# The first loads of weights issued behind the first pair's queries, keys and values

## The chip, the core and the metric

One Trainium2 chip, and on it one core. The metric is the time of one execution of the whole program on the device, in microseconds (us). The core's engines are TensorE (PE, with its weight loads as PEld), VectorE (DVE), ScalarE (ACT), GpSimd (POOL) and SyncE (SP); SP issues every transfer of this kernel.

## What is computed

A layer of attention with a memory beside it, and a gated layer of experts' size behind it, all in 32-bit floats:

```
a     = softmax(mask(q k^T / 8));  local = a v                 # B=4, H=8, S=576, D=64
q_p   = phi(q);  mem = (q_p M_prev) / (q_p z_prev + 1e-6)      # phi(x) = max(x + 1, exp(min(x, 0)))
x     = sigmoid(beta) * mem + (1 - sigmoid(beta)) * local      # -> 2304 x 512
out   = (sigmoid(x w_gate) * (x w_val)) w_out                  # 512 -> 1536 -> 512
```

## The kernel before

The 2304 rows of x are worked in six groups of 384. For each group, attention is computed for four pairs of heads, in three items each; the first group takes the tails (192 queries) of two batches, so a pair of it has two loads of queries and keys (`kp`), two of values (`vt` or `vr`) and shares two tiles of the memory (`mb`). The expert layer of a group (`moe`) runs over 12 blocks f of 128 hidden columns, and while it runs the attention of the next group is woven into it.

The weights arrive as 64-bit numbers. For a block f three raw tiles of 512 KB (`wr`, three buffers) are loaded, and `convert` turns each into a high and a low 32-bit part: one operation on ACT (line 603), four on DVE (604, 606, 609, 612), a copy on ACT (223) and a subtraction on DVE (233). One result stays in `wg`, a tile per f; the other two go to `sv`, which has three buffers, and are also written to `w` in device memory, from where later groups load them. So the conversion of 36 raw tiles goes on beside the attention and the experts of group 0, and f+3 needs an `sv` buffer that the experts' block f has left.

Every operation is first recorded with its engine and its dependences (`Program.add`), and `issue` then orders them: it plays the program with costs from a table and gives each engine, whenever it is free, the ready operation with the lowest number `order`. That number is the place at which the operation was recorded, less a lead from the table `LEAD`: loads and stores of weights on SP have a lead of 200. The order on each engine is fixed when the kernel is built; on the chip, each engine takes its instructions in that order and waits at one whose inputs are not there. The first block's weights are recorded inside the first attention pair (behind its eighth step), the second's behind the 22nd, the others from inside `moe`. The first pair's recorded operations begin with the loads of `kp` (numbers 4 and 5), `bt`, `vt`, the next pair's `kp` and the `mb` tiles (18 to 22, with POOL's clearing of them between).

Of the kernel before, what the change touches and what calls it, by code (L numbers as in the profile page):

```python
# [25 lines left out]
COLD = 12.0  # L26

LEAD = {("attention", "pe"): 150, ("weights", "sp"): 200}

WAKE = {  # L30
    "act": {"act": 0.14, "dve": 0.13, "pe": 0.26, "pool": 0.2, "sp": 0.14},
# [7 lines left out]
class Program:  # L39
# [24 lines left out]
    def add(self, engine, cost, emit, reads=(), writes=(), kb=0):  # L64
        i = len(self.ops)
        deps = set()
        for k in (*reads, *writes):
            if k[:2] in self.touched:
                use, ops = self.touched[k[:2]]
                assert use == k[2], f"{k} is read or written after its buffer went to a new use"  # L70
                if k in writes and k not in self.writer:
                    deps.update(self.before[k[:2]])
                ops.add(i)
        for k in reads:
            if k in self.writer:
                deps.add(self.writer[k])
        for k in writes:
            if k in self.writer:
                deps.add(self.writer[k])
            deps.update(self.readers.pop(k, ()))  # L80
        for k in reads:
            self.readers.setdefault(k, set()).add(i)
        for k in writes:
            self.writer[k] = i
        deps.discard(i)
        order = (i if self.turn is None or engine != "pe" else self.turn) - LEAD.get((self.part, engine), 0)
        self.ops.append((engine, cost, kb, emit, deps, order))

    @contextmanager
# [712 lines left out]
```

## Time and profile before

| | |
|---|---|
| median of 3 runs | 687.88 us (686.35 to 690.77) |
| the profiled execution | 686.17 us, its span 684.4 us |
| PE busy / PEld busy | 663.3 us (97%) / 582.0 us (85%) |
| DVE / ACT / POOL busy | 363.1 / 334.3 / 8.1 us |
| granted clock of TensorE, mean | 0.999 |
| moved | 122.20 MB, mean 179 GB/s |

The span is the time between the first and the last recorded instruction. The busy share of PE is a mean over all stages; PE's ends are modelled, so that short waits between matmuls don't appear as idle time. Rows of a timeline start with the start in us and the length in us; a row in brackets at the end tells how long the engine was idle before and what released it. SPq rows are SP's issues of transfers, not the transfers themselves.

### The profile page before, as it was taken

Reading aid. Unit: us, or ns where it says so; the run is one execution under the profiler, and the core shown is the slowest. Engines: PE = TensorE matmul, PEld = TensorE weight load, DVE = VectorE, ACT = ScalarE, POOL = GpSimd, SP = SyncE. Lnnn points to the kernel's source line nnn. Section 1 sums busy time; section 2 is a strip of 40 time slices with the busy share of each in tenths; the row PEclk is TensorE's granted clock in tenths of the full one; section 3 lists DMA queues with packets and bytes.
Section 4 is the critical chain, followed back from the end, with each engine's and each line's share of the span. In section 5 each row is a group of like instructions: output and inputs, shape, how many; then the busy total and the mean of one; then the engine's idle time right before and its main releaser. Section 6 shows DMA issues by size and latency. Waiting matters only on the chain.

```text
span 684.4 us, 12496 instructions
## 1 busy us (share of the span) xinstructions
PE 663.3 (97%) x4992; PEld 582.0 (85%) x4992; DVE 363.1 (53%) x995; ACT 334.3 (49%) x656; POOL 8.1 (1%) x52
## 2 busy tenths in 40 slices
PE   4999999999999999999999999999999999999996
PEld 2556688887799999899999999989998899999995
DVE  6799889898864443454444345454445533111111
ACT  6678656557663553553454454354644624121111
POOL 2000000000000000000000000000000000000000
PEclk9999999999999999999999999999999999999999
DMA  8677757877644543543444634543622331554541
GB/s 280 238 260 239 231 157 260 271 235 267 230 153 162 178 169 140 197 155 136 167 147 143 266 117 162 180 168 125 241 102 92 134 124 63 185 186 167 185 168 63
DMA packets 31946, 122.20 MB, mean 179 GB/s; under 512 B 7568, under 2 KB 9616, under 8 KB 22672
## 3 DMA queue, kind: packets, MB, share of 16 engines
q1 hardware_dynamic: 31888, 121.41, 51.1%
q8 instruction: 39, 0.64, 0.4%
q14 instruction: 19, 0.16, 0.1%
HBM read 104.09 MB, written 17.30 MB: 177 GB/s over the span
## 4 chain that ended last, share of the span: by engine, by line
PE 90%; ACT 5%; DMA 2%; DVE 1%; issue 1%; SPq 1%; POOL 0%; ACTq 0%
PE bank L210 70%; PE bank L214 10%; PE bank L217 7%; PE bank L472 4%; ACT a L493 1%; ACT kq L223 1%; DMA vt<-in_vp_dram 1%; ACT at L223 1%; DMA kp<-in_qk_dram 1%; SPq L241 1%; DVE a L484 0%; ACT wt L603 0%; DMA out_dram<-ob 0%; ACT ob L704 0%; DVE xs L233 0%
## 5 line engine op out<-in xcount | busy, mean ns | idle before, releaser
L210 PE MATMUL bank<-xh,sv 128*128 128x384 f32 x576 | 169.4, 347 | 0.1
L210 PE MATMUL bank<-xh,wg 128*128 128x384 f32 x576 | 166.0, 343 | 0.3
L210 PE MATMUL bank<-sv,gh 128*128 128x512 f32 x432 | 142.6, 407 | 0.0
L689 DVE SCALAR_TENSOR_TENSOR th<-th,bank 128x384 f32<-128x384 f32 x72 | 39.8, 553 | 145.3 <-PE bank L210 130.7
L210 PEld LDWEIGHTS bank<-xh,wg 128*128 128x128 f32 x576 | 105.1, 188 | 7.8 <-issue 2.9
L210 PEld LDWEIGHTS bank<-xh,sv 128*128 128x128 f32 x576 | 105.8, 188 | 3.7 <-issue 1.8
L493 ACT ACTIVATE a<-a,st 128x512 f32<-128x512 f32 (+4 forms) x144 | 79.8, 581 | 44.7 <-DVE st L484 43.7
L687 ACT ACTIVATE th<-bank 128x384 f32<-128x384 f32 x72 | 35.3, 490 | 133.8 <-PE bank L210 133.5
L210 PE MATMUL bank<-xl,sv 128*128 128x384 f32 x288 | 98.0, 340 | 0.0
L210 PE MATMUL bank<-xl,wg 128*128 128x384 f32 x288 | 98.0, 340 | 0.0
L484 DVE CUSTOM_DVE_ANT_0 a<-bank,mask 128x512 f32<-128x512 f32 (+4 forms) x144 | 66.5, 485 | 55.6 <-PE bank L210 49.3
L210 PEld LDWEIGHTS bank<-sv,gh 128*128 128x128 f32 x432 | 78.0, 188 | 13.1 <-issue 0.7
L210 PE MATMUL bank<-sv,gl 128*128 128x512 f32 x216 | 87.4, 405 | 0.0
L217 PE MATMUL bank<-idn,a 128*128 128x128 f32 x400 | 73.2, 278 | 3.8 <-ACT a L493 2.8
L223 ACT COPY at<-bank 128x512 f32<-128x512 f32 (+1 forms) x120 | 59.1, 514 | 34.7 <-PE bank L217 34.6
L223 ACT CAST gh<-th 128x384 fp32r<-128x384 f32 x72 | 36.9, 512 | 62.9 <-DVE th L689 62.2
L217 PEld LDWEIGHTS bank<-idn,a 128*128 128x128 f32 x400 | 49.7, 142 | 15.0 <-ACT a L493 4.9
L210 PEld LDWEIGHTS bank<-xl,wg 128*128 128x128 f32 x288 | 54.2, 188 | 3.0 <-issue 0.5
L223 ACT CAST kq<-kp 64x768 fp32r<-64x768 f32 (+1 forms) x76 | 48.2, 638 | 16.4 <-PE bank L210 15.2
L210 PEld LDWEIGHTS bank<-xl,sv 128*128 128x128 f32 x288 | 54.2, 188 | 1.0 <-issue 0.7
L472 PE MATMUL bank<-kp 64*128 64x512 f32 (+5 forms) x156 | 42.1, 494 | 9.4 <-DMA kp<-in_qk_dram 8.4
L233 DVE TENSOR_TENSOR gl<-th,gh 128x384 fp32r<-128x384 f32 x72 | 39.9, 554 | 20.5 <-ACT gh L223 20.1
(62 smaller groups left out, 693.2 us busy)
## 6 DMA issues: line engine op xcount, KB each, us to landing
sv<-w SPq DMA_DIRECT2D x60, 1024.0 KB, 4.8
wr<-in_w_dram SPq DMA_DIRECT2D x36, 512.0 KB, 4.4
kp<-in_qk_dram SPq DMA_DIRECT2D x32, 384.0 KB, 4.8
w<-sv SPq DMA_DIRECT2D x12, 1024.0 KB, 4.8
out_dram<-ob SPq DMA_DIRECT2D x16, 256.0 KB, 4.4
vt<-in_vp_dram SPq DMA_DIRECT2D x8, 330.0 KB, 4.1
vr<-in_vp_dram SPq DMA_DIRECT2D x8, 330.0 KB, 5.7
vt<-in_vp_dram SPq DMA_DIRECT2D x8, 198.0 KB, 3.2
```

Of the source, the lines that this page charges most:

```text
L210: lambda: nc.tensor.matmul(out=out, lhsT=lhsT, rhs=rhs, start=start, stop=stop), r, w)
L214: lambda: nc.tensor.matmul(out=out, lhsT=lhsT, rhs=rhs, start=start, stop=stop), r, w)
L217: pe(0.110, lambda: nc.tensor.transpose(out=out, in_=in_, identity=identity), r, w)
L223: act(n, lambda: nc.scalar.copy(out=out, in_=in_), r, w)
L233: dve(n, lambda: nc.vector.tensor_tensor(out=out, in0=in0, in1=in1, op=op), r, w)
L241: pg.add("sp", 0.5, lambda: nc.sync.dma_start(out=out, in_=in_), r, w, kb)
L472: pe(2 * m / 2385.0, lambda kp=kp, j=j, r=r, q=q, m0=m0, m1=m1: nc.tensor.matmul(out=sp[j][0][m0:m1, :m], lhsT=kp[r, u.qa + q:u.qa + q + m ...
L484: dve(m + 60, lambda aj=aj, sj=sj, pj=pj: nc.vector.tensor_tensor_reduce(out=aj[:, k0:k1], in0=pj[:, :m], in1=mk, scale=-0.125, scalar=3.0 ...
L493: act(W, lambda aj=aj, sj=sj: nc.scalar.activation(out=aj[:, :W], in_=aj[:, :W], func=AF.Exp, scale=-1.0, bias=sj[:, len(ns) - 1:len(ns)], ...
L687: act(GT, lambda: nc.scalar.activation(out=th, in_=pg_[:, :GT], func=AF.Tanh, scale=0.5), [pg_k], [th_k])
L689: dve(GT, lambda: nc.vector.scalar_tensor_tensor(out=th, in0=th, scalar=1.0, in1=pv[:, :GT], op0=ALU.add, op1=ALU.mult,), [th_k, pv_k], [t ...
```

## The change

A lower bound is put on the number that orders loads and stores of weights on SP. Before, the lead of 200 made the numbers of the first block's loads negative, and they stood ahead of every other transfer. Now no such number is below 21, which is the number of the third of the four loads of the `mb` tiles.

```diff
 LEAD = {("attention", "pe"): 150, ("weights", "sp"): 200}
+
+FIRST = 21
@@ Program.add
         deps.discard(i)
+        first = FIRST if (self.part, engine) == ("weights", "sp") else -1000
         order = (i if self.turn is None or engine != "pe" else self.turn) - LEAD.get((self.part, engine), 0)
+        order = max(order, first)
         self.ops.append((engine, cost, kb, emit, deps, order))
```

Nothing else of the source changes; line numbers behind `Program.add` grow by four. Since `issue` plays the whole program, the order on all engines moves.

On SP, the start of the program. `wr` are the raw weights, `kp` queries and keys, `bt` the gate's numbers, `vt` values. A wait on DMAHW is one for an earlier transfer to have landed: there are eight such counters, and a transfer waits for the one eight places ahead of it. Before:

```order
L241 DMA wr_129<-in_w_dram 128x1024
L241 DMA wr_131<-in_w_dram 128x1024
L241 DMA wr_133<-in_w_dram 128x1024
L241 DMA kp_101<-in_qk_dram 128x768
L241 DMA kp_102<-in_qk_dram 128x768
L241 DMA bt<-in_beta_dram 128x8
L241 DMA vt_103<-in_vp_dram 128x660
L241 DMA vt_104<-in_vp_dram 128x660
L241 DMA kp_105<-in_qk_dram 128x768 [waits DMAHW0_49]
```

The same place of the changed kernel, from its first transfer on:

```order
L245 DMA kp_101<-in_qk_dram 128x768
L245 DMA kp_102<-in_qk_dram 128x768
L245 DMA bt<-in_beta_dram 128x8
L245 DMA vt_103<-in_vp_dram 128x660
L245 DMA vt_104<-in_vp_dram 128x660
L245 DMA kp_105<-in_qk_dram 128x768
L245 DMA kp_106<-in_qk_dram 128x768
L245 DMA mb_107<-in_mz_dram 64x4x65 [waits Pool_49]
L245 DMA mb_107<-in_mz_dram 64x4x65 [waits DMAHW0_49]
L245 DMA mb_108<-in_mz_dram 64x4x65 [waits DMAHW1_49,Pool_49]
L245 DMA wr_129<-in_w_dram 128x1024 [waits DMAHW2_49]
L245 DMA wr_131<-in_w_dram 128x1024 [waits DMAHW3_49]
```

The three loads of raw weights went from the first three places to the 11th to 13th; the last quarter of `mb` and the next pair's values follow them.

On DVE, its first instructions. `wt` is the working tile of a conversion; rows 484 (488 after) read the first scores out of a bank. Before:

```order
L604 TENSOR_SCALAR wt_130<-wt_130 128x512
L606 TENSOR_SCALAR wt_130<-wt_130 128x512
L609 SCALAR_TENSOR_TENSOR wt_130<-wr_129,wt_130 128x512
L612 SCALAR_TENSOR_TENSOR wt_130<-wr_129,wt_130 128x512
L604 TENSOR_SCALAR wt_132<-wt_132 128x512
...
L612 SCALAR_TENSOR_TENSOR wt_132<-wr_131,wt_132 128x512
L606 TENSOR_SCALAR wt_134<-wt_134 128x512
L484 ISA a_112,st_114<-bank_63,mask 128x512
```

In the changed kernel DVE begins with that last row, and its first conversion stands behind the first pair's first two items (from the 14th row on):

```order
L488 ISA a_123,st_124<-bank_70,mask 128x320
...
L488 ISA a_123,st_124<-bank_64,mask_73,st_124 128x256
L488 ISA st_124 128x1
L608 TENSOR_SCALAR wt_130<-wt_130 128x512
L610 TENSOR_SCALAR wt_130<-wt_130 128x512
L488 ISA a_113,st_114<-bank_68,mask 128x512
L488 ISA st_114 128x1
L488 ISA a_118,st_115<-bank_69,mask 128x512
L488 ISA st_115 128x1
L613 SCALAR_TENSOR_TENSOR wt_130<-wr_129,wt_130 128x512
```

Eleven rows of conversion went from ahead of the first score to between the scores of the first pair and behind them.

On PE, the first products with the memory (`mb`, with the features `ph`) among the scores (`kp`) and transposes (`idn`). Before:

```order
L472 MATMUL bank_64<-kp_102 64x256
L217 MATMUL bank_66<-idn,a_118 128x128 x4
L217 MATMUL bank_67<-idn,a_119 128x128 x3
L214 MATMUL bank_65<-mb_107,ph_109 128x130
L217 MATMUL bank_67<-idn,a_119 128x128
L472 MATMUL bank_68<-kp_105 128x512
```

After:

```order
L476 MATMUL bank_70<-kp_102 64x320
L218 MATMUL bank_65<-mb_107,ph_109 128x130
L476 MATMUL bank_63<-kp_102 64x320
L476 MATMUL bank_64<-kp_101 64x256
L476 MATMUL bank_64<-kp_102 64x256
L221 MATMUL bank_66<-idn,a_118 128x128 x4
```

The product with `mb` stands about ten matmuls earlier. From the experts' first block of group 1 on, all engines have the same order in both kernels (on DVE from just behind the 36th and last conversion).

## Rows read from the trace of the kernel before

**Rows 1.** The page, part 1: busy time, share of span and instructions of each engine.

```profile
PE 663.3 (97%) x4992; PEld 582.0 (85%) x4992; DVE 363.1 (53%) x995; ACT 334.3 (49%) x656; POOL 8.1 (1%) x52
```

**Rows 2.** Busy time by stretch: stretch, length, engines' busy us, granted clock, DMA share, GB/s.

```profile
0.00:5.50 5.50, 0.00 (x0) 0.00 (x0) 0.00 (x0) 1.94 (x2) 4.43 (x20) 1.00 0.66 212
5.50:14.00 8.50, 5.15 (x14) 2.33 (x15) 8.35 (x23) 5.29 (x11) 0.24 (x2) 1.00 0.91 328
14.00:30.00 16.00, 14.65 (x108) 8.53 (x108) 11.82 (x37) 12.07 (x25) 0.23 (x2) 1.00 0.82 269
30.00:60.00 30.00, 28.73 (x325) 17.48 (x322) 27.68 (x86) 23.44 (x47) 0.47 (x4) 1.00 0.67 225
60.00:100.00 40.00, 38.39 (x420) 30.34 (x416) 33.94 (x98) 24.73 (x51) 0.59 (x5) 1.00 0.66 210
100.00:172.50 72.50, 71.60 (x455) 59.69 (x452) 66.79 (x162) 47.00 (x92) 0.22 (x2) 1.00 0.76 253
172.50:200.00 27.50, 27.28 (x225) 22.93 (x226) 19.80 (x57) 17.16 (x34) 0.22 (x2) 1.00 0.65 226
200.00:684.40 484.40, 477.55 (x3468) 440.67 (x3467) 194.75 (x537) 202.65 (x399) 1.69 (x15) 1.00 0.43 153
```

**Rows 3.** Waits of PE, first 60 us: line, waited for, us, times, longest.

```profile
PE bank L472 <- DMA kp<-in_qk_dram: 8.4, 1, 8.4
```

**Rows 4.** Timeline, first 10 us: SP's first issues, and who starts when they land.

```profile
0.73 1.35 SPq L241 DMA_DIRECT2D wr<-in_w_dram  x3
2.13 1.14 SPq L241 DMA_DIRECT2D kp<-in_qk_dram  x2
4.82 0.66 ACT L603 ACTIVATE wt<-wr 128x512 f32<-128x512 f32 x1 [2.81 <-DMA wr<-in_w_dram]
6.07 0.67 ACT L603 ACTIVATE wt<-wr 128x512 f32<-128x512 f32 x1 [0.59 <-DMA wr<-in_w_dram]
8.38 3.79 PE L472 MATMUL bank<-kp 64*128 64x512 f32 x8 [8.38 <-DMA kp<-in_qk_dram]
9.40 0.34 PEld L472 LDWEIGHTS bank<-kp 64*128 64x128 f32 x2 [0.51 <-DMA kp<-in_qk_dram]
```

**Rows 5.** Loads of kp, first 30 us, six of them: from issue to landing.

```profile
DMA to landing us min/median/max: 3.5/6.4/9.0
```

**Rows 6.** Timeline, DVE: its first instruction, and the first score.

```profile
5.51 0.43 DVE L604 TENSOR_SCALAR wt<-wt 128x512 f32<-128x512 f32 x1 [5.51 <-ACT wt L603]
11.05 0.68 DVE L484 CUSTOM_DVE_ANT_0 a<-bank,mask 128x512 f32<-128x512 f32 x1
```

**Rows 7.** Transposes on PE by shape, from 8 to 14.2 us, then 14.2 to 30 us.

```profile
L217 PE MATMUL bank<-idn,a 128*128 128x128 f32 x7 | 1.8, 423 | 0.5 <-POOL vt L374 0.5
...
L217 PE MATMUL bank<-idn,a 128*128 128x128 f32 x35 | 5.3, 287 | 1.3 <-ACT a L493 1.3
```

**Rows 8.** The conversions' last operation on DVE, first 200 us: duration, first and last start.

```profile
L612 DVE SCALAR_TENSOR_TENSOR wt<-wr,wt x36: 651/684/697, 7.2 to 174.4; 128x512 int32<-128x512 int32 x36
```

**Rows 9.** Waits of DVE from 5.5 to 172.5 us, the two longest sums.

```profile
DVE wt L604 <- ACT wt L603: 9.3, 6, 5.5
DVE a L484 <- PE bank L472: 5.5, 12, 1.0
```

**Rows 10.** Timeline: block 0's weights ready and first used, then block 11's.

```profile
8.57 0.68 DVE L233 TENSOR_TENSOR wg<-wt,wg 128x512 fp32r<-128x512 f32 x1
...
64.26 0.42 PE L210 MATMUL bank<-xh,wg 128*128 128x384 f32 x1
...
171.81 0.69 DVE L233 TENSOR_TENSOR wg<-wt,wg 128x512 fp32r<-128x512 f32 x1
172.56 0.62 PE L210 MATMUL bank<-xh,wg 128*128 128x384 f32 x2
```

**Rows 11.** The mb tiles, first 30 us: products on PE; from issue to landing.

```profile
L214 PE MATMUL bank<-mb,ph x16: 274/275/378, 16.4 to 22.7; 128*128 128x130 f32 x12, 128*64 128x130 f32 x4
...
DMA to landing us min/median/max: 5.9/7.2/8.1
```

## The prediction

> **What bounds the kernel now.** I read the page's busy shares first: PE is busy for 97% of the span [rows 1], so the question is where the other 3% lies and whether the change reaches it. The table by stretch answers that [rows 2]. PE does nothing for the first 5.5 us and little until 14; from 14 to 172.5 us it is idle for 5.1 us in all (1.35 + 1.27 + 1.61 + 0.90, each stretch's length less its busy time); from 200 us on it is as good as always busy up to the last stores. The one long wait is the first: 8.4 us until the first queries and keys land [rows 3]. The timeline shows why they come so late [rows 4]: SP issues three raw weight loads first (0.73 us), the first `kp` at 2.13 us. ACT starts on the first raw tile at 4.82 us and on the second at 6.07 us, 1.25 us apart; PE starts at 8.38 us and waits once more, until 9.40 us, for the second `kp`. The transfers land one behind another, at 384 KB in 1.02 us.
>
> The second thing to see is DVE. In the stretch in which PE waits, DVE is not idle: it converts weights from 5.51 us on and comes to the first scores only at 11.05 us [rows 6]. From 5.5 to 172.5 us it is busy for 8.35 + 11.82 + 27.68 + 33.94 + 66.79 = 148.6 us of 167, so 18.4 us idle [rows 2]. And the weights, which are 55 us early for block 0 (ready at 8.57 + 0.68 = 9.25 us, used from 64.26 us on), are just in time for block 11: DVE finishes a part at 171.81 + 0.69 = 172.50 us and PE takes it at 172.56 us [rows 10]. The conversion loses against PE over the first group, so up to about 172 us DVE and PE share the bound. Behind the last conversion (its last long operation starts at 174.4 us [rows 8]) the order on all engines is the same before and after, and PE is the bound there. So whatever PE has won or lost by then goes to the end one for one.
>
> **The change, part by part.**
>
> The first `kp` is issued at 0.73 us instead of 2.13 us, with nothing ahead of it. Its landing has two rows as bounds: the quickest of six `kp` loads took 3.5 us [rows 5], which gives 4.2 us; the first load of before, the raw tile, took 4.82 - 0.73 = 4.1 us [rows 4], and 128 KB less are worth 0.34 us at 384 KB in 1.02 us, which gives 4.5 us. I take 4.45 us, nearer to the row of the same place in the program. PE starts 3.9 us earlier (bounds 3.9 to 4.2).
>
> The Trainium skill, in DMA: Bandwidth & Descriptors, section Anatomy of one DMA, puts a transfer at about 2.0 us and its bytes at 436 GB/s, which for 393,216 bytes is 2.9 us, and the start at 3.6 us. The section's fit is for transfers that GpSimd issues; here SP does, and no row is that quick. By it the sum below would be 0.8 us lower, 684.6 us.
>
> DVE's first read of scores follows the first product by 1.1 to 1.2 us (a product of this kind takes 1.02 us at that place [rows 4], and an engine is released within 0.1 us [rows 4, 6, 10]), so at 5.6 us instead of 11.05 us: the eleven rows of conversion ahead of it are gone. For a while PE wins more than 3.9 us. Against that stands `mb`: its first product stands about ten matmuls earlier in PE's order, and everything behind waits with it. I estimate its tile behind five loads of 1.02 or 0.88 us (4.8 us from 4.45 on), the short `bt` and its own short pieces, at 11 us; that is the least sure number, since in the trace these pieces took 5.9 to 8.1 us from issue to landing and their product ran at 16.4 us [rows 11]. PE would come to it at about 10 us, and wait 1 us (0 to 2). So PE is some 3 to 4 us ahead at the end of the first items.
>
> The raw tiles now queue behind seven to ten loads. The first lands at about 13 us (11 us plus 1.25 us, and the release of SP between) instead of 4.8 us. Block 0 has 55 us in hand, so this costs nothing there [rows 10]. But the work does not go away: the eleven rows that took DVE from 5.51 to 11.05 us, 5.5 us, now stand between the scores that PE waits for. Here the account of DVE's time decides. DVE starts at 5.6 us instead of 5.5, and up to the last conversion it has the same work. So it can be there earlier only by being idle for less than 18.4 us. Two terms:
>
> - More idle time early. Up to about 13.3 us DVE has only seven reads of scores at up to 0.68 us [rows 6], the features and small rows, an estimate of 6 us of work; so it is idle for 1.7 us of 7.7, against 0.15 us (8.50 less 8.35) now [rows 2]. With the later start that is +1.7 us.
> - Less idle time later. The 5.5 us owed can be done in gaps. Gaps now: 4.2 us from 14 to 30 us, 2.3 to 60, 6.1 to 100, 5.7 to 172.5 [rows 2]. The long waits are for raw tiles by way of ACT (9.3 us, of which 5.5 are the start) and for scores [rows 9]. Bounds: nothing of it fits (0) and all of it fits (-5.5). I take the gaps from 14 to 30 us alone, 4.2 us, in which the tiles that landed at 13 to 16 us are at hand; what is owed beyond that falls into stretches in which DVE is 92 to 94% busy.
>
> Sum: +1.7 - 4.2 = -2.5 us at 172 us, bounds +1.7 and -3.8. PE's own account agrees: 3 to 4 us won, about 1 us given back to scores that come later behind conversions. The profiled execution took 686.17 us, so 683.7 us; it lies 1.7 us under the median of the runs (687.88 us), and with that offset the sum is 685.4 us. The bounds are 684.1 and 689.6 us on the same scale. One per cent, 6.9 us, is about what a measurement of this kernel can tell from no change (the three runs lie 4.4 us apart).
>
> **The rivals.**
>
> *All is kept.* The whole 5.5 us fits into gaps, and PE holds the 3.9 us of its start: 684.0 us. For it: 18 us of gaps, and PE idle for 5.1 us in the same stretches, a part of which may go too. Against: DVE is 92% busy from 30 to 60 and from 100 to 172.5 us, and the gaps there are waits for PE, which move with PE.
>
> *All is given back.* Block 11's weights are ready when they are now, since the conversions are paced by three raw buffers and by DVE, not by PE: 687.9 us. For it: no slack at block 11 [rows 10]. Against: conversions from block 3 on need `sv` buffers that PE's earlier blocks leave, so they move with PE too.
>
> *Slower: the conversions become late.* Only the early idle time counts, and less than 1.7 us of what is owed finds a gap. Then DVE finishes block 11's weights up to 1.7 us later, at 174.2 us, PE stands at block 11 for so long, and the time is up to 689.6 us. The point from which it decides is 1.7 us of gaps filled; 14 to 30 us alone has 4.2.
>
> *The clock takes the gain.* PE's 128x128 transposes take 423 ns up to 14.2 us and 287 ns after [rows 7]; that looks like the lower and the upper of its two levels, 1.2 and 2.4 GHz, though the granted-clock column reads 1.00 in both [rows 2]. PE had been idle for 8.4 us before the first of them. If the lower level lasts to 14.2 us again, PE works up to 14.2 - 4.45 = 9.75 us at it instead of 5.8, and loses half of the difference, up to 2.0 us: 685.4 + 2.0 = 687.4 us. Against: before that, PE waits for `mb` and DVE anyway.
> The Trainium skill, in TensorE: Matmul & The Clock Gate, section Part 1, says that the throttled state is the default and activity releases it; by that rule the release moves with PE's start, and this rival falls away. No row here shows which.
>
> That the change does nothing can be left out: the first load on SP is another.
>
> **How the numbers follow.** The forecast (1 to 3.6 us faster) has 0.50; all kept (3.6 to 6) 0.20; given back or taken by the clock (1 us either way) 0.20; slower (1 to 4) 0.10. The range from 682 to 689 us takes in the first three and the runs' own scatter of about 1.5 us, and leaves out the far ends of the first and last rival. Faster by over 1% (under 681.0 us) would need 6.9 us, more than the start holds: 0.05 with PE's other waits gone as well. Slower by over 1% would need more than four times the price of the slower rival: 0.03. Within 1%: 0.92.
>
> **What would show it.** In the changed kernel's profile: PE's first matmul at 4.2 to 4.5 us; DVE's first row a read of scores at about 5.6 us; the first conversion on DVE behind 13 us; a wait of PE at the first `mb` product of up to 2 us; block 11's last weights and PE's use of them at 169 to 171 us; the stretch from there to the end as long as now. The forecast is wrong if block 11's weights are ready at 172 us or later, or if PE stands for more than 2 us anywhere between 14 and 170 us.

## The result, and the profile after

The changed kernel is slower: 694.98 us median of 4 runs (693.80 to 695.93) against 687.12 us for the kernel before in the same comparison (685.70 to 690.77). The ratio is 1.0107, 95% interval 1.0077 to 1.0137. The forecast was 685.4 us, range 682 to 689; the result lies 9.6 us above it and 6 us above the range. One run of `e3_before_early_pe` (698.17 us) and one of the kernel before (1056.80 us) count as slow and are left out of the medians and ratios below.

The profiled execution has a span of 694.1 us against 684.4 us, so 9.7 us more (it is the longest of the four changed runs, 692.0 to 694.1 us; the medians of the times lie 7.9 us apart). Part 1 of its page, in the form of [rows 1]:

```profile
PE 672.3 (97%) x4992; PEld 586.0 (84%) x4992; DVE 362.0 (52%) x995; ACT 335.1 (48%) x656; POOL 8.0 (1%) x52
```

This line has one half of the answer. The same 4992 matmuls keep PE busy for 672.3 us instead of 663.3, which is 9.0 us more; PE's idle time, span less busy, went from 21.1 to 21.8 us, only 0.7 us more. The other engines are as busy as before. PE did the same work more slowly. The idle time hides the other half: at its start PE stands 4.13 us instead of 8.38, so behind its start it stands 21.8 - 4.13 = 17.7 us instead of 21.1 - 8.38 = 12.7, which is 5.0 us more. Where, the table by stretch says (the columns and stretches of [rows 2], changed kernel):

```profile
0.00:5.50 5.50, 1.37 (x4) 0.84 (x6) 0.00 (x0) 2.01 (x3) 3.54 (x17) 1.00 0.55 151
5.50:14.00 8.50, 5.81 (x25) 2.79 (x24) 4.41 (x17) 5.46 (x11) 1.06 (x5) 0.94 1.01 301
14.00:30.00 16.00, 13.16 (x55) 7.25 (x55) 12.24 (x35) 10.19 (x19) 0.23 (x2) 0.71 0.59 188
30.00:60.00 30.00, 28.88 (x310) 18.03 (x310) 21.77 (x68) 17.92 (x36) 0.23 (x2) 0.89 0.63 220
...
200.00:694.10 494.10, 487.29 (x3568) 449.66 (x3566) 200.64 (x556) 208.39 (x413) 1.81 (x16) 1.00 0.43 154
```

The granted clock, 1.00 in every stretch of [rows 2], is now 0.94, 0.71 and 0.89 from 5.5 to 60 us. From 14 to 30 us PE gets through 55 matmuls in 13.16 busy us; before it was 108 in 14.65 (in another order, so not the same ones). Cut where the clock changes, the same view of the changed kernel reads:

```profile
4.10:9.50 5.40, 5.33 (x16) 2.75 (x16) 3.14 (x12) 3.19 (x7) 0.93 (x7) 1.00 0.83 256
9.50:12.90 3.40, 0.97 (x8) 0.20 (x6) 0.64 (x4) 2.94 (x7) 0.37 (x2) 1.00 1.12 256
12.90:19.80 6.90, 6.68 (x24) 3.69 (x25) 3.02 (x11) 3.02 (x6) 0.23 (x2) 0.51 0.80 265
19.80:26.60 6.80, 5.02 (x29) 2.81 (x28) 6.45 (x18) 4.52 (x8) 0.00 (x0) 1.00 0.26 77
26.60:36.80 10.20, 9.13 (x93) 6.27 (x95) 6.74 (x20) 5.00 (x11) 0.00 (x0) 0.50 0.77 285
36.80:60.00 23.20, 22.08 (x228) 13.19 (x226) 18.43 (x57) 15.62 (x30) 0.23 (x2) 1.00 0.62 206
```

TensorE is at its upper level (2.4 GHz) from 9.5 us, falls to the lower (1.2 GHz) at 12.9 us, is up at 19.8, falls again at 26.6 and is up from 36.8 us until the last stores. (The column reads 1.00 until its first change, so the start up to 9.5 us, which is at the lower level by the length of its transposes, 409 ns, doesn't show in it.) In the two low stretches PE is busy for 6.68 + 9.13 = 15.8 us. Ahead of each fall PE had been waiting. Its waits in the first 60 us of the changed kernel (columns of [rows 3]):

```profile
PE bank L476 <- DMA kp<-in_qk_dram: 4.8, 3, 4.1
PE bank L218 <- DMA mb<-in_mz_dram: 2.6, 1, 2.6
PE bank L221 <- ACT a L497: 2.1, 2, 1.8
PE bank L476 <- DVE xm L237: 0.8, 1, 0.8
...
```

The 8.4 us at the start became 4.1; in its place stand 2.6 us for `mb`, 1.8 us for a row of scores from ACT, and shorter ones. The timeline of the changed kernel shows their places (rows of PE, DVE and SP's issues, up to 38 us):

```profile
0.73 0.88 SPq L245 DMA_DIRECT2D kp<-in_qk_dram  x2
4.13 3.78 PE L476 MATMUL bank<-kp 64*128 64x512 f32 x8 [4.13 <-DMA kp<-in_qk_dram]
6.36 0.69 DVE L488 CUSTOM_DVE_ANT_0 a<-bank,mask 128x512 f32<-128x512 f32 x1 [6.36 <-PE bank L476]
6.79 2.86 SPq L245 DMA_DIRECT2D wr<-in_w_dram  x3
10.51 0.54 SPq L245 DMA_DIRECT2D mb<-in_mz_dram  x1
13.12 0.77 PE L218 MATMUL bank<-mb,ph 128*128 128x130 f32 x2 [2.64 <-DMA mb<-in_mz_dram]
...
24.98 0.65 PE L476 MATMUL bank<-kp 64*64 64x256 f32 x4 [0.81 <-DVE xm L237]
27.46 1.33 PE L221 MATMUL bank<-idn,a 128*128 128x128 f32 x5 [1.83 <-ACT a L497]
29.00 1.22 PE L476 MATMUL bank<-kp 64*128 64x512 f32 x1 [0.20 <-DMA kp<-in_qk_dram]
...
32.26 5.39 PE L218 MATMUL bank<-vt,at 128*64 128x66 f32 x104
```

Three quarters of `mb` are issued ahead of the raw weights, the last one behind them, at 10.51 us. The first product with `mb` comes at 13.12 us after 2.64 us of waiting. In PE's order the products that need the last quarter stand far behind it, at 21.57 us. They are not waiting for the transfer there: no load of `mb` took longer than 8.5 us to land, so it is in by 19.0 us, and PE reaches them without a wait for it. It is the order that `issue` made for the later transfer that puts them so late. In the kernel before they ran at 17.88 us, and the products with the values that come up below took 3.25 us:

```profile
17.88 1.08 PE L214 MATMUL bank<-mb,ph 128*128 128x130 f32 x6
...
29.09 3.25 PE L214 MATMUL bank<-vt,at 128*64 128x66 f32 x104
```

The chain of waits (start, us, what) shows what hangs on them in the changed kernel:

```profile
21.57 1.02 PE bank L218 x6
22.59 0.02 issue
22.62 0.17 DVE rn L402
22.78 0.33 DVE wt L608
23.11 0.10 DVE rn L404
23.21 0.57 DVE wt L613
23.78 0.07 DVE rn L237
23.86 0.60 DVE wg L237
24.46 0.48 DVE xm L237
24.94 0.04 issue
24.98 0.67 PE bank L476 x4
25.65 3.30 DMA kp<-in_qk_dram
```

The products run at 21.57 us, DVE makes `rn` (factors of the rows) and `xm` (the memory's part of x) out of them with three rows of conversion in between, only then is the bank free for the first pair's last scores (24.98 us), and only when these are done is their buffer free for the next load of `kp`, issued at 25.65 us and used at 29.00 us. The kernel before issued that load at 24.64 us, with a PE that had begun 4.25 us later. All of it then runs into the second low stretch: the 104 short products with the values (`vt`, `at`), 3.25 us before, take 5.39 us at 32.26 us.

The weights fall behind with the rest. Block 11's last part on DVE, in the timeline of the changed kernel (in the form of [rows 10]):

```profile
181.57 0.68 DVE L237 TENSOR_TENSOR wg<-wt,wg 128x512 fp32r<-128x512 f32 x1
```

The last of the conversions' long operations starts at 184.8 us instead of 174.4 us [rows 8]. Block 11 is ready at 182.25 us instead of 172.50 us: 9.75 us late, as much as the whole loss of the profiled span. From 200 us on PE's rate is what it was.

### The profile page after: what moved, and what is told of

It is laid out like the page before. It is cut to its first block, busy times and chain, and to the rows that moved or that the text cites. A ratio compares the mean times of both kernels' runs of the same rounds, so it can differ in the third digit from the quotient of the medians.

```text
span 694.1 us, 12486 instructions
## 1 busy us (share of the span) xinstructions
PE 672.3 (97%) x4992; PEld 586.0 (84%) x4992; DVE 362.0 (52%) x995; ACT 335.1 (48%) x656; POOL 8.0 (1%) x52
## 4 chain that ended last, share of the span: by engine, by line
PE 91%; ACT 4%; DMA 3%; DVE 1%; POOL 0%; issue 0%; SPq 0%; POOLq 0%; ACTq 0%; DVEq 0%
PE bank L214 69%; PE bank L218 10%; PE bank L221 7%; PE bank L476 5%; DMA kp<-in_qk_dram 2%; ACT kq L227 1%; DMA mb<-in_mz_dram 1%; ACT a L497 1%; ACT at L227 0%; DMA out_dram<-ob 0%; ACT gh L227 0%; ACT wt L607 0%; ACT sv L227 0%; ACT th L691 0%; DVE wt L613 0%
## 5 line engine op out<-in xcount | busy, mean ns | idle before, releaser
L488 DVE CUSTOM_DVE_ANT_0 a<-bank,mask 128x512 f32<-128x512 f32 (+3 forms) x144 | 66.7, 486 | 68.2 <-PE bank L214 49.1
L221 PE MATMUL bank<-idn,a 128*128 128x128 f32 x400 | 74.7, 283 | 3.0 <-ACT a L497 2.1
L221 PEld LDWEIGHTS bank<-idn,a 128*128 128x128 f32 x400 | 51.1, 145 | 15.5 <-issue 4.5
L227 ACT CAST kq<-kp 64x768 fp32r<-64x768 f32 (+2 forms) x76 | 48.2, 638 | 17.4 <-PE bank L214 15.2
L476 PE MATMUL bank<-kp 64*128 64x512 f32 (+5 forms) x156 | 44.8, 533 | 6.1 <-DMA kp<-in_qk_dram 4.8
```

What stands on the lines that cost most here:

```text
L221: pe(0.110, lambda: nc.tensor.transpose(out=out, in_=in_, identity=identity), r, w)
L227: act(n, lambda: nc.scalar.copy(out=out, in_=in_), r, w)
L476: pe(2 * m / 2385.0, lambda kp=kp, j=j, r=r, q=q, m0=m0, m1=m1: nc.tensor.matmul(out=sp[j][0][m0:m1, :m], lhsT=kp[r, u.qa + q:u.qa + q + m ...
L488: dve(m + 60, lambda aj=aj, sj=sj, pj=pj: nc.vector.tensor_tensor_reduce(out=aj[:, k0:k1], in0=pj[:, :m], in1=mk, scale=-0.125, scalar=3.0 ...
```

## The experiments

Two theories were put against each other. **A**: a stretch in which PE stands idle makes the granted clock fall, and the low clock costs the time. **B**: the time is lost because inputs come late, that is, because of the conversions that now stand between the scores on DVE and because of the late `mb`; the clock adds little. Where a kernel has dummy products, they multiply the identity into columns of a bank that nobody reads or that are overwritten, so PE is busy while it waits; everything else keeps its order. A dummy is two matmuls in the profile. "Span" is that of the profiled execution; medians come with the ratio to the kernel before in the same comparison and its 95% interval.

**The first wait filled** (`e1_fill_wait`: twelve dummies ahead of the first product with `mb`).

```diff
+FILL = 12
...
+                    for _ in range(FILL):
+                        nc.tensor.matmul(out=t[:, 390:510], lhsT=idn, rhs=idn[:, :120], start=True, stop=True)
```

> The changed kernel with twelve extra products of the identity tile (128x120, into columns of the bank that nothing reads) put on PE directly ahead of the first product with mb, where PE stands idle for 2.64 us in the changed kernel; the order of everything else on all engines is the same. Theory A (the idle stretch makes the clock fall, and the low clock costs the time): the granted clock stays at its upper level from about 9.5 us to at least 20 us, the products of that stretch take half as long, and the kernel takes 690 to 693.5 us instead of 695; if the second low stretch (26.6 to 36.8 us) goes with it, down to 687. Theory B (the time is lost to the conversions that now stand between the scores on DVE, and to the wait for mb itself; the clock is a by-product): the wait for mb lasts as long, only filled, and the time stays within 1 us of 695.

Measured: 692.80 us, 1.0104 (1.0066 to 1.0141); span 690.3 us. By stretch:

```profile
8.90:25.90 17.00, 13.82 (x91) 8.82 (x89) 12.65 (x38) 12.12 (x23) 0.75 (x5) 1.00 0.81 236
25.90:32.80 6.90, 6.58 (x66) 4.11 (x68) 4.58 (x16) 3.63 (x9) 0.00 (x0) 0.51 0.86 336
```

The fall at 12.9 us is gone and the second low stretch is 6.9 us long instead of 10.2. The span is 3.8 us shorter and the median 2.2 us; 692.80 us lies in A's range and outside B's, but the ratio is not clearly lower than the changed kernel's. The clock fell again at 25.9 us, behind the waits for `xm` and the late row of scores.

**Dummies for the later waits too** (`e5_fill_three`: the twelve, and 3, 7 and 3 more, meant for the three waits between 22 and 27 us).

> The changed kernel with 12 dummy products ahead of the first mb product and 3, 7 and 3 more at the three places between 22 and 27 us where PE stood waiting (for a score's bank, for a0 at its transposes, for the next pair's kp). The order of everything else is that of the changed kernel; the dummies write bank columns that are overwritten before they are read. Theory A (an idle stretch of PE makes the granted clock fall, and the low clock costs the time): with the four waits filled the clock rises once and stays; against the run with only the first wait filled (690.3 us span, 692.8 us median) another 3 to 4 us go, so about 688 to 690 us. Theory B (the conversions that now stand between the scores on DVE, and the late mb, cost the time by themselves): PE's true work comes when its inputs come, dummies or not, so within 1 us of the run with one fill, 692 to 694 us.

Measured: 691.67 us, 1.0070 (1.0045 to 1.0095); span 690.0 us. The edit did not do all that was meant. Only the seven stand at their wait, ahead of the transposes of the late row of scores. The other two threes came to stand at 13.88 and 34.77 us, where PE had no wait, and the waits for `xm` and for `kp` are unfilled:

```profile
13.88 0.93 PE L219 MATMUL bank<-idn 128*128 128x120 f32 x6
...
23.40 0.65 PE L497 MATMUL bank<-kp 64*64 64x256 f32 x4 [0.81 <-DVE xm L246]
23.98 1.82 PE L219 MATMUL bank<-idn 128*128 128x120 f32 x14
...
27.64 1.81 PE L497 MATMUL bank<-kp 64*128 64x512 f32 x6 [0.98 <-DMA kp<-in_qk_dram]
...
34.77 0.83 PE L219 MATMUL bank<-idn 128*128 128x120 f32 x6
```

PE's busy time is, dummies included, hardly less than in the changed kernel (part 1 of the page):

```profile
PE 671.4 (97%) x5042; PEld 587.1 (85%) x5042; DVE 362.0 (52%) x995; ACT 334.7 (49%) x656; POOL 8.0 (1%) x52
```

The clock stays up all the same, from 5.5 to 14 us too (table by stretch):

```profile
14.00:30.00 16.00, 14.12 (x98) 8.67 (x100) 12.93 (x37) 11.72 (x22) 0.23 (x2) 1.00 0.67 213
30.00:60.00 30.00, 28.88 (x325) 18.25 (x320) 25.41 (x79) 20.70 (x39) 0.47 (x4) 1.00 0.67 222
```

The dummies are 6.5 us of it (2.9 and 3.6 us by line), so the kernel's own work took 664.9 us, nearly the 663.3 us of before. Nearly all that PE was slower at is the clock. But idle time and dummies together are now 690.0 - 664.9 = 25.1 us against 21.8: of the 7.4 us that the clock gave back 3.3 us did not reach the end, and up to 1.8 us of these are the six dummies that fill no wait. So the clock is worth 4.1 us of span here (3.3 us between the medians), or up to 5.9 us, an estimate, if those 1.8 us counted in full; 5.6 us of the loss stand with the clock up. Against one fill the span fell by 0.3 us and the median by 1.1 us, where A had said 3 to 4; neither range held, and B's number was the nearer.

**The last quarter of `mb` ahead of the raw weights too** (`e2_behind_mb`).

```diff
-FIRST = 21
+FIRST = 23
```

> The bound on the number of weight transfers is 23 instead of 21, so that the three raw loads stand behind all four loads of mb; the planner then puts the products with both mb tiles together at the same early place on PE. Theory A: PE still stands idle at the first product with mb, for 2.6 to 4 us, the clock falls there too: 692 to 697 us. Theory B: conversions start 0.5 us later at most, so the time stays at 694 to 697 us. If the place of the last quarter of mb behind the raw loads is what costs (it lands late and PE waits at its product): 3 us or more under 695.

Measured: 688.34 us, 1.0015 (0.9992 to 1.0038); span 687.8 us. One transfer of 65 KB, moved past three others, with the order that follows from it on all engines, is worth 6.3 us of span and 6.6 us between the medians, as the third of the expected outcomes had it; transfer and order are not told apart. All of the first pair's products with `mb` now run in one piece at 13.03 us, `xm` is ready at 18.2 us, the next `kp` is issued at 20.83 us instead of 25.65 us, and between 20 and 37 us there is no low clock and one wait, of 0.7 us. The wait at `mb` itself stays (2.7 us, and with it a low stretch), and a second fall comes at 81.1 us:

```profile
12.90:19.70 6.80, 6.67 (x26) 4.10 (x26) 2.77 (x11) 2.59 (x6) 0.23 (x2) 0.50 0.67 258
...
81.10:87.90 6.80, 6.80 (x57) 5.13 (x57) 4.48 (x13) 2.79 (x6) 0.11 (x1) 0.50 0.42 137
```

**Both: all of `mb` ahead, and its wait filled** (`e7_behind_mb_fill`: `FIRST = 23` and the twelve dummies).

> The bound raised by two, so that the raw weights stand behind all four mb loads (as in an earlier run, 688.3 us), and 12 dummy products ahead of the first mb product, so that PE doesn't stand idle there; the order of everything else as in that run. Theory A: the low stretch of the clock from 12.9 to 19.7 us goes, which is worth 2 to 4 us: 684.5 to 686.5 us, the first version that would not be slower than before. Theory B: the scores and conversions on DVE set the pace there, so the same time as without the dummies, 687.5 to 689 us.

Measured: 686.34 us, 0.9985 (0.9964 to 1.0006); span 684.8 us. A was right in place and size. Four kernels now make a square, with one edit along each side: the changed kernel, `e1_fill_wait`, `e2_behind_mb` and this one. The place of the last quarter of `mb` costs 6.3 us of span without dummies (694.1 against 687.8) and 5.5 us with them (690.3 against 684.8). The unfilled wait at `mb`, with the low clock behind it, costs 3.8 us (694.1 against 690.3) and 3.0 us (687.8 against 684.8). Either way round they add up to 9.3 us of the 9.7 us. Between the medians they are 6.6 and 6.5 us, 2.2 and 2.0 us. In the ratios the place of `mb` is clear of the intervals in both rows, the dummies in neither.

The record has the mean granted clock of every run, and it shows the clock's price a second way. Of the ten runs of this version the four at 0.997 or more have spans of 681.6 to 683.8 us, the six at 0.993 or 0.994 have 684.5 to 687.0 us. Of 83 runs of the kernel before, the 61 at 0.997 or more have a median span of 684.7 us, the 8 at 0.993 one of 687.2 us. So with the same instructions in the same order an execution with a mean clock lower by about 0.005 is some 2.5 us longer, in the kernel before too. That the clock alone makes this difference is not shown: a late input could make both a wait and a fall. The profiled executions of `e2_behind_mb` and of this version hold a late fall that those of the changed kernel and of `e1_fill_wait` don't, so the price of `mb` above is, if anything, too low.

Of the late fall, here from 79.3 to 86.1 us, and what stood ahead of it:

```profile
76.00:79.30 3.30, 2.36 (x10) 1.38 (x10) 3.30 (x13) 1.50 (x4) 0.11 (x1) 0.99 0.77 278
79.30:86.10 6.80, 6.80 (x60) 5.68 (x59) 4.70 (x13) 2.58 (x5) 0.11 (x1) 0.50 0.33 100
```

**That late fall too** (`e9_fill_late`: 3 and 3 dummies at the two waits of 0.47 us ahead of it).

> The version with the raw weights behind all four mb loads and 12 dummy products ahead of the first mb product (686.3 us; its clock fell once more, from 79.3 to 86.1 us, behind two waits of PE of 0.47 us each at 76 to 78 us), with 3 and 3 dummy products more at those two waits; the rest of the order is the same. Theory A (the falls of the clock behind short waits are a large part of the loss): the stretch from 79.3 to 86.1 us goes to the upper level, in which PE was busy for 6.8 us at the lower, so 2.5 to 3.4 us go: span 681 to 682.5 us, median 682.5 to 684 us, faster than both kernels. Theory B (what counts is when the inputs come): within 1 us of the version without them, 685.5 to 687 us.

Measured: 686.29 us, 1.0003 (0.9980 to 1.0026); span 683.6 us. In the profiled execution the clock is up from 7.6 to 680 us, and still the span is only 0.8 us shorter than before's. The dummies took 1.9 us where the waits had taken 0.94 us. A's 2.5 to 3.4 us were missed: the span fell by 1.2 us, the median not at all, and the 12 runs lie between 684.3 and 692.9 us. Neither does the forecast come true here, with `mb` in time and the clock up: PE starts at 4.07 us, 4.3 us earlier than before, but up to 62 us its idle time (8.1 us) and the twelve dummies (2.9 us) are 11.0 us against 11.5 us of idle time in the kernel before. Waits for later inputs have taken all but 0.5 us of the early start by then.

**Fewer conversions on DVE** (`e6_less_dve` in the changed kernel, `e10_fill_less_dve` in the version with all of `mb` ahead and filled, `e11_before_less_dve` in the kernel before). Of the four operations, the last three are left out, for block 0 alone:

```diff
-        dve(DM, lambda: nc.vector.tensor_scalar(
+        dve(DM, lambda: f and nc.vector.tensor_scalar(
```

> The changed kernel, with three of the four first operations on DVE left out (those that sort out the two 32-bit parts) in the conversion of block 0's three raw tiles alone: nine instructions, about 5.4 us of DVE, so that block 0's weights are not the reference's; order and waits of the rest are as in the changed kernel. Theory B: it is these instructions between the scores and the gate's rows that made a0 and the xm rows late; then the waits of 0.81 and 1.83 us at 24 to 27 us go and the end comes 4 to 6 us earlier, 689 to 691 us. Theory A: the wait at the first mb product and the first low stretch of the clock stay (13 to 20 us); the end comes at most 2 us earlier, 693 to 695 us, unless the waits at 24 to 27 us go and with them the second low stretch.

> The version with the raw weights behind all four mb loads and the 12 dummies (686.3 us, span 684.8 us), leaving out three of the four first operations on DVE in the conversion of block 0's raw tiles alone (nine instructions, some 5.4 us of DVE; block 0's weights are not the reference's). Theory B: the owed conversions, now between the scores, cost PE time up to 60 us; without them the time falls by 3 to 5 us, to 681.5 to 683.5 us. Theory A: with mb in time and the clock up, PE's early pace is set by its own work and by the late falls of the clock; within 1.5 us of the version with them, 685 to 687.5 us.

> Control: the kernel before, with the same nine instructions of block 0's conversion left out (block 0's weights are not the reference's). In before six of them stand ahead of the first scores on DVE. If DVE sets the pace at the start (what both theories now hold), the first scores are read at 9 to 9.5 us instead of 11.05 us and the end comes 1 to 2.5 us earlier, 684 to 686 us; if the owed work is only worth something between the scores, no change, 686 to 687.5 us.

Measured: `e6_less_dve` 693.08 us, 1.0086 (1.0059 to 1.0113), span 691.0 us, 3.1 us less than with them; only one fall of the clock is left, at 26.2 us, and the wait for the row of scores is still 1.43 us. But this execution differs from the changed kernel's before the first instruction that is left out: ACT waits 2.4 us for `bt` instead of 1.0 us, PE's first transposes start at 9.14 us instead of 7.96, the clock comes up at 12.5 us instead of 9.5, and PE waits 1.2 us at `mb` instead of 2.64. So its 3.1 us can't be put down to the conversions, and the 1.9 us between the medians are within the intervals. `e10_fill_less_dve` 686.31 us, 0.9971 (0.9950 to 0.9993), span 684.6 us, against 686.34 us, 0.9985 and 684.8 us with them; among the four runs of each at a mean clock of 0.997 or more its spans are 680.2 to 681.6 us against 681.6 to 683.8. `e11_before_less_dve` 687.02 us, 1.0003 (0.9991 to 1.0014); its first scores are read at 10.53 us, behind PE and not behind DVE. So with `mb` in time the owed conversions, the half of B on which my account rested, cost nothing that is clear of the scatter, at most some 1.5 us; what they cost with `mb` late stays open. The other half of B, the late `mb`, is what stood in the square above.

**Other places for the raw weights** (`e4_behind_kp`: `FIRST = 6`, behind the first pair's `kp` and `bt` alone; `e8_mb_first`: `FIRST = 23` and the loads of `mb` ahead of the next pair's `kp`).

> The bound is 6 instead of 21: the three raw loads stand behind the first pair's two kp loads and the gate's numbers alone, ahead of the values, the next pair's kp and mb. The products with mb then stand later in PE's order, behind the scores of the next pair. Theory A: PE starts at 4.1 us as in the changed kernel, finds no wait of 2 us at mb, the clock does not fall again, and the time is 683 to 686 us, under before. Theory B: the conversions start about 2.5 us later than before and about 3 us of them are owed between the scores: 688 to 691 us.

> As the run with the raw weights behind all four mb loads, and the mb loads of the first unit recorded ahead of the second pair's queries and keys, so that mb lands about 2 us earlier, at 10.5 to 11.5 us. Theory A: the wait of PE at the first mb product shrinks from 2.7 us to under 1 us, the clock doesn't fall there, and the time is 684 to 686 us. Theory B: mb lands early as well and DVE gets its features earlier, but the conversions still stand between the scores: 687 to 689 us, with the lag growing again after 70 us.

Measured: `e4_behind_kp` 691.73 us, 1.0075 (1.0054 to 1.0097), span 689.5 us; waits for rows of scores of 3.6 us, and the clock low from 26.8 to 30.2 and from 43.8 to 50.6 us. `e8_mb_first` 690.70 us, 1.0053 (1.0033 to 1.0073), span 687.2 us: there is no wait for `mb`, but 1.54 us ahead of the first transposes, and PE works at the lower level up to 16.5 us. Neither theory's range held in either run. Both have a late `bt` in them: ACT waits for it 2.9 and 2.6 us (1.0 us in the changed kernel) and makes its first rows of scores behind it, and PE's first transposes wait 1.78 and 1.54 us for these rows. `bt` is the third transfer in all of them, and in `e6_less_dve`, with the changed kernel's order, ACT's wait for it was 2.4 us; so part of what these two runs show is how one transfer varies from one execution to the next. With five dummies at that wait (`e12_mb_first_fill`):

> The version with mb ahead of the next pair's keys (690.7 us; the profiled run had a span of 687.2 us, TensorE at the lower level up to 16.5 us, and PE idle for 1.54 us at 7.7 to 9.2 us, ahead of the first transposes), with 5 dummy products at that wait; the rest of the order is the same. Theory A (it was the idle stretch that kept the clock down to 16.5 us): the clock is up by 8 to 9 us; PE was busy for 7.4 us from 7.6 to 16.5 us at the lower level, so 2 to 3.5 us go, a span of 684 to 685 us, and with no later fall the version could be up to 1 us under the kernel before. Theory B (DVE and ACT set the pace of the first items): PE waits longer for a0 and the scores' banks instead, 0 to 1 us gained, 686.5 to 687.5 us of span.

Measured: 688.10 us, 1.0016 (1.0000 to 1.0033); span 686.5 us. The clock is up at 9.8 us, 6.7 us earlier, and the span shrinks by 0.7 us only: PE comes earlier and waits 2.0 us for copies from ACT, where it had waited 1.0 us. B's number held for the span. Between the medians it is 2.6 us, inside A's 2 to 3.5, with intervals that just touch; the profiled execution of `e8_mb_first` is one of its fastest (688.97 us).

**The start of the kernel before at the upper level** (`e3_before_early_pe`: 16 dummies at PE's start, from 1.36 us).

> The kernel before with sixteen extra products of the identity tile (128x120, into a bank that the first scores overwrite) at the start of PE's order, from about 1.4 us on, while it waits for the first kp; all else in the same order. Theory A (low clock costs PE time at the start): the clock is at its upper level when the first scores start at 8.4 us, the four products then take half as long, and the kernel is 1 to 2.7 us faster than before, 684.5 to 686. Theory B (DVE sets the pace at the start, since it reads the first scores at 11.05 us whatever PE does): 0 to 0.5 us faster, 686.5 to 687.

Measured: 687.49 us, 1.0013 (0.9997 to 1.0029); span 687.1 us. Timeline of PE:

```profile
8.24 2.07 PE L478 MATMUL bank<-kp 64*128 64x512 f32 x8 [0.28 <-DMA kp<-in_qk_dram]
12.41 0.66 PE L219 MATMUL bank<-idn,a 128*128 128x128 f32 x4 [2.10 <-ACT a L499]
...
27.73 3.46 PE L219 MATMUL bank<-idn,a 128*128 128x128 f32 x15 [1.35 <-ACT a L499]
```

The first scores take 2.07 us instead of 3.79 us [rows 4], and PE then stands for 2.10 us: its first transposes start at 12.41 us instead of 12.64. So the low clock at the start costs the kernel before next to nothing by itself; PE waits for its inputs there. And the clock fell twice more (14.0 to 17.4 and 27.7 to 31.1 us), the second time behind a wait of 1.35 us that the kernel before has as well, without a fall.

No version that does all of the work beat the kernel before by more than its measurement tells.

## Why the prediction was wrong, point by point

The step that failed is what the new order does to PE by way of `mb`. The prediction counted one wait of 1 us (0 to 2) at the first product and nothing for the last quarter of `mb` behind the raw weights; the place of that quarter was worth 5.5 to 6.3 us of span. The second step that failed is the rival on the clock, priced at up to 2.0 us and let go; it was worth 3 to 4 us in the profiled executions and some 2 us between the medians.

- **PE's start**: right. 4.13 us, 4.25 us earlier than before; predicted 4.45 us. By the fit of the Trainium skill (DMA: Bandwidth & Descriptors, Anatomy of one DMA), which is for transfers that GpSimd issues, an estimate for this one was 2.9 us and a start at 3.6 us. From its issue to PE's start it took 3.4 us, so the neighbouring rows were nearer.
- **DVE's first read of scores at 5.6 us**: 6.36 us. The first instruction on DVE is a read of scores, as the order said; it came 2.2 us behind PE's start instead of 1.1 to 1.2. The 1.02 us taken from [rows 4] are a wait for the second `kp`, not the length of a product: the row has eight matmuls for four scores. In `e11_before_less_dve`, with DVE free, the first read also comes 2.2 us behind PE's start (8.30 and 10.53 us).
- **The raw tiles at 13 us, conversions on DVE behind them**: ACT takes the first tile at 14.46 us, DVE at 16.00 us. Right in kind, 1.5 us late, and as the runs without these conversions show, of no weight that is clear of the scatter once `mb` is in time.
- **The wait at the first `mb` product, "1 us (0 to 2)"**: 2.64 us, outside its bounds. The estimate of the landing, 11 us, was made from the big tiles' rows; the loads of `mb` themselves took 7.4 to 8.5 us from issue to landing, and the chain of waits has the one that PE waited for landing at 12.87 us. [rows 11] had 5.9 to 8.1 us; from the issue at 4.78 us that alone gives 10.7 to 12.9 us.
- **"everything behind waits with it"** was written of the first product only. That the last quarter went behind the raw weights stands in the order that I showed, and I gave it no price. It was 5.5 to 6.3 us, the largest single term: the rest of the first pair's products with `mb`, `xm`, the bank, the first pair's last scores, and the buffer of the next `kp` hang on it one behind another. With its first `mb` product PE is still 3.3 us ahead of the kernel before (13.12 against 16.40 us [rows 11]), as forecast; with the rest of the pair's products it is 3.7 us behind (21.57 against 17.88 us).
- **DVE's account, +1.7 and -4.2 us**: wrong in both terms. From 5.5 to 14 us DVE is idle for 8.50 - 4.41 = 4.1 us, 3.9 more than before, not 1.7. From 14 to 30 us it is idle for 3.76 us instead of 4.18 us, so that 0.4 us of the gaps was used, not 4.2; and from 30 to 60 us for 8.23 us instead of 2.32. DVE had time for the conversions; it was waiting for PE. (The "92 to 94% busy" behind 30 us also passes over the stretch from 60 to 100 us, 85% by [rows 2].) Its waits for scores, 5.5 us in [rows 9], are now, from 5.5 to 182 us:

```profile
DVE a L488 <- PE bank L476: 16.6, 14, 6.4
```

- **The rival "the clock takes the gain", up to 2.0 us**: the right mechanism, mis-sized. It priced only how long the first low stretch lasts. The clock came up at 9.5 us, earlier than before's 14.2 us. The Trainium skill (TensorE: Matmul & The Clock Gate, Part 1) says that the throttled state is the default and activity releases it, and the first rise of the trace agrees. I let the rival fall away on that without asking what each new wait would do. The clock fell twice, PE's own work took 9.0 us longer, 3.8 us of the span came back with the first wait filled, and 4.1 us with the clock up throughout.
- **The rival "the conversions become late", up to 689.6 us**: the sign was right, the reason is not what the runs show. Leaving nine of them out changed nothing clear of the scatter once `mb` was in time.
- **Block 11 at 169 to 171 us; wrong if at 172 us or later, or if PE stands for over 2 us**: 182.25 us, so the first test caught it. The second did not: it asked for a wait between 14 and 170 us, and the longest there was 1.83 us. The wait of 2.64 us ended at 13.12 us; it breaks the "up to 2 us" for the first `mb` product.

What stays open: the profile is of one execution. The mean clock of the others is on record, but not where they have their falls. The runs of one version with dummies lie 1.8 to 8.6 us apart, those of the kernel before 3.2 to 5.1 us. The 5.5 to 6.3 us for the last quarter of `mb` come from four kernels and agree in both directions and in the medians; how they are divided between the transfer, the order made for it and the links of its chain was not measured. The 3 to 4 us for the wait with the low clock behind it come from single executions and are not clear of the intervals in the ratios.

## What to carry to other kernels

When the loads at a kernel's start are put in a new order, follow every tile of the first unit of work to its first use, the last piece of each above all: one small transfer left behind three large ones, with the order made for it, cost more here than the start had won. A new wait of PE early on is to be priced twice, once as idle time and once as matmuls at the lower level behind it, and the granted clock by stretch belongs beside the waits when the two traces are compared. Where busy time grows with the same instructions and idle time doesn't, look at the clock before looking for contention or for a busy engine.

## What the runs showed of the hardware

- TensorE's clock, once up, fell again while PE was partly busy. PE was busy for 0.97 of 3.40 us ahead of the fall at 12.9 us, for 5.02 of 6.80 us ahead of that at 26.6 us, and for 2.36 of 3.30 us, with two waits of 0.47 us, ahead of that at 79.3 us. The same wait of 1.35 us stood ahead of a fall in one kernel (`e3_before_early_pe`) and of none in another (the kernel before), and in `e5_fill_three` waits of 0.81 and 0.98 us had none behind them; so the length of the last wait alone doesn't decide.
- The first rise is not tied to PE's start, which was at 3.9 to 4.3 us in these versions. Where PE did not wait ahead of its first transposes it came at 7.6 us (`e7_behind_mb_fill`) to 10.5 us (`e10_fill_less_dve`); where it waited 1.2 to 1.8 us there, at 12.5 us (`e6_less_dve`), 13.1 us (`e4_behind_kp`) and 16.5 us (`e8_mb_first`).
- A transfer of 4 KB (`bt`), the third to be issued, varied by over a microsecond: ACT waited for it 0.5 us in `e7_behind_mb_fill`, 1.0 us in the changed kernel, and 2.4 us in `e6_less_dve`, whose order is the changed kernel's.
- Four loads of 65 KB in short pieces (`mb`) took 7.4 to 8.5 us from issue to landing, behind five loads of 330 or 384 KB and more; the first `kp`, 384 KB with nothing ahead of it, let PE start 3.4 us after its issue.
